# Retention and a Gelu MLP on one core: constants made earlier, seven warm-up matmuls, one load moved ahead, and a choice of queue for the last stores

## The chip, the cores and the metric

The kernel runs on one core of a Trainium2 chip. The metric is the device time of one execution in microseconds (us). The core has a matrix engine (TensorE, PE in the profile, with its weight loads shown apart as PEld), three engines for elementwise work (VectorE as DVE, ScalarE as ACT, GpSimd as POOL) and SyncE (SP), which here only issues transfers. Each engine runs its own list of instructions in a fixed order and waits on semaphores for the others.

## The reference

Inputs are q, k and v of shape (batch 8, heads 8, sequence 576, head size 64) and two weight matrices, 512 x 2048 and 2048 x 512, all float32. Each head is retention without a softmax: scores with a decay by distance, below the diagonal only. The heads side by side form 4608 rows of 512, which go through an MLP with an exact Gelu.

```python
scores = scale * np.matmul(q, k.transpose(0, 1, 3, 2))
gamma = 1.0 - 2.0 ** (-5.0 - np.arange(H, dtype=np.float32))
Dmat = np.where(rel >= 0, gamma[:, None, None] ** rel[None, :, :], 0.0)
x = rows_of(np.matmul(scores * Dmat, v))          # (4608, 512)
out = gelu_exact(x @ w_in) @ w_out                # (4608, 512)
```

## The kernel before, in words

The sequence is cut in chunks of 128 positions, with a last chunk of 64. A unit is one chunk of one batch element, or two last chunks of 64 together; there are 36 units of 128 rows. For a unit, q and k are turned to have the head dimension on the partitions (`qkT`), the scores are taken per head in PSUM (`sc`), VectorE multiplies them by a mask (`ret`, line 452), and a matmul with v gives the unit's result (`o_ps`, line 489). From the second chunk on, an accumulated state of k and v (`u_ps`, `u_sb`) is multiplied by q and added (line 560). First chunks use masks `near` that hold the decay itself. Later chunks use a plain 0/1 mask `msk`, with v scaled by `dv` (`vh`, line 463) and the result by `dqT` (line 583). Four units make a block `x` of 512 tokens, of which there are nine.

The MLP of a block is a first layer (`hT`, line 603, then Gelu into `g_all`) and a second layer (`oT`, line 636, or `fa` and `fb`, line 707). From the second block on the second layer, and for the last three blocks the first layer too (`ha`, `hb`, line 812), use Strassen-like sums with seven products in place of eight, whose operands VectorE prepares (`s`, `wt`, `ws`, `x_sum`).

The order of every engine's instructions is fixed while the program is written, by a planner in the kernel. It keeps an estimated clock per engine (the dictionary `T`), estimated landing times of transfers (`land`), and a main loop that picks what TensorE does next: attention steps that are estimated as ready come first, and otherwise pieces of the MLP. So a changed estimate near the start can move matmuls of the MLP ahead of or behind attention steps much later. Where nothing is estimated as ready before 16 us, `warm(n)` (line 1020) puts matmuls on a tile of zeros into the gap; lines 1048 to 1051 put eight of them ahead of everything.

What the change touches lies at the two ends:

- Lines 108 to 110 load q and k of the first unit as float32, q by SyncE's queue and k by ScalarE's. They are cast to bf16 by VectorE (line 333 is the helper that records such copies on VectorE, line 335 on ScalarE). All other loads are issued by GpSimd in the order of the list `ORDER` (line 281): `wi` is a piece of w_in (256 columns), `wo` a piece of w_out, `q1`, `k1`, `v1` belong to unit 1, and `io` stands for the constants' positions.
- `constants()` makes `val`, `far`, the eight `near` tiles (by exponentials on ScalarE, line 154) and `ident`. The rest (`make_args`, `make_msk`, the exponentials `dv` and `dqT`, and one Gelu on a single column that loads ScalarE's table) lies in a list `later`, from which the main loop takes an item when its planned time has come (lines 174 to 184 and 996 to 1003).
- `put()` (line 1014) issues the stores of a finished tile of 128 rows on SyncE's queue. A unit made of two last chunks has two stores of 64 rows each.

Of the kernel before, what the change touches and what calls it, by code (L numbers as in the profile page):

```python
# [11 lines left out]
AF = mybir.ActivationFunctionType  # L12
# [5 lines left out]
def kernel(  # L18
# [14 lines left out]
    nc = tc.nc  # L33
    ctx.enter_context(tc.manual_schedule())

    B, H, S, D = q.shape
# [3 lines left out]
    scale = 1.0 / math.sqrt(D)  # L40
    HP = H // 2
# [4 lines left out]
    N_BLK = n_tok // TOK  # L46
# [23 lines left out]
    N_LD = 5  # L70
    N_QKT = 3
    N_KN = 4
    VH_POOL = 26
    N_VH = 6
    N_XB = 4
# [3 lines left out]
    HOT = 7.5  # L79
# [16 lines left out]
    T = dict.fromkeys(("pe", "act", "dve", "pool", "sp"), 0.0)  # L96
# [11 lines left out]
    for nm, src, eng in (("q32", q, nc.sync), ("k32", k, nc.scalar)):  # L108
        t = first[nm] = o_pool.tile([128, H, D], FP32, tag="o_sb", name=nm)
# [6 lines left out]
    ln_scale = const.tile([128, 1], FP32, name="ln_scale")  # L116
# [13 lines left out]
    pe_arg = const.tile([128, H, NCI], FP32, name="pe_arg")  # L130
    dv = const.tile([128, H, NCI], FP32, name="dv")
    off = const.tile([128, HP, 1], FP32, name="off")
    dqT = const.tile([128, HP, S - C], FP32, name="dqT")
    warm_act = const.tile([128, 1], FP32, name="warm_act")
# [10 lines left out]
    def constants():  # L145
        nc.gpsimd.iota(val[:, 0, :], pattern=[[1, 128]], base=0, channel_multiplier=-1,
                       allow_small_or_imprecise_dtypes=True)
        nc.gpsimd.iota(pos[:, 0, :], pattern=[[C, NCI]], base=0, channel_multiplier=1,
                       allow_small_or_imprecise_dtypes=True)
        at = on("pool", 0.45)  # L150
        nc.vector.tensor_scalar(far, val, 0.0, 1.0e6, op0=ALU.is_lt, op1=ALU.mult)
        nc.vector.tensor_tensor(far, far, val, op=ALU.add)
        for h in range(H):
            nc.scalar.activation(near[:, h % 2, h // 2], far[:, 0, :], AF.Exp, scale=log_gamma[h], bias=ln_scale)
        nc.vector.tensor_scalar(ident, val, 0.0, None, op0=ALU.is_equal)
        T["act"] = at + 0.6 + H * 0.27
        T["dve"] = at + 0.9

    ident1 = ident[:, 0, :]

    def make_args():
        nc.vector.tensor_scalar(pos[TAIL:, :, NCI - 1:], pos[TAIL:, :, NCI - 1:], float(-TAIL), None, op0=ALU.add)
        nc.vector.tensor_tensor(pe_arg, lgh.to_broadcast([128, H, NCI]), pos.to_broadcast([128, H, NCI]), op=ALU.mult)
        nc.vector.tensor_tensor(off, lgT, pos[:, :, 1:2].to_broadcast([128, HP, 1]), op=ALU.mult)
# [6 lines left out]
    def make_dq(hp):  # L171
        nc.scalar.activation(dqT[:, hp, 0:C], val[:, 0, :], AF.Exp, scale=lgT[:, hp], bias=off[:, hp])

    later = [(7.6, "dve", 0.45, make_args), (7.6, "dve", 0.6, make_msk),
             (8.5, "act", 0.3, lambda: nc.scalar.activation(dv, pe_arg, AF.Exp, scale=-1.0, bias=ln_scale))]
    later += [(9.0, "act", 0.41, lambda hp=hp: make_dq(hp)) for hp in range(HP)]
    later += [(9.0, "act", 1.45, lambda: nc.scalar.activation(warm_act, ln_scale, AF.Gelu))]
    T["act"], T["dve"], T["pool"] = 2.6, 2.9, 0.85

    def finish_later():  # L180
        while later:
            _, engine, dur, fn = later.pop(0)
            fn()
            on(engine, dur)
# [6 lines left out]
    land = {}  # L191
# [37 lines left out]
    def load(what, i):  # L229
# [37 lines left out]
        for jj in (j,) if j is not None else range(2):  # L267
# [5 lines left out]
            else:  # L273
# [2 lines left out]
            land[what, i] = sw_dma(0.9, 0.9) if j is not None else sw_dma(0.68, 0.5)  # L276

    tiles_of(0)
    land["q", 0], land["k", 0] = 4.5, 4.6
    cast_due = {("q", 0): (loaded[0][0][:, 0], first["q32"]), ("k", 0): (loaded[0][0][:, 1], first["k32"])}  # L280
    ORDER = ("wi0 io k1 q1 v0 v1 wi1 q2 k2 v2 wi2 k3 q3 v3 wi3 wi4 wi5 wi6 wi7 wo0 wo1 wo2 wo3 wo4 wo5 wo6 wo7 "
             "q4 k4 q5 k5 v4 v5 dq2 q6 k6 q7 k7 v6 v7 q8 k8 q9 k9 v8 v9 dq3 q10 k10 v10 dq4 q11 k11 q12 k12 n11 n12 v11 v12").split()

    def next_order():
# [39 lines left out]
    def pe(dur, to="full"):  # L324
        if mode[0] != to:
            T["pe"] += 0.11
            mode[0] = to
        T["pe"] += dur * (2.0 if T["pe"] < HOT else 1.0)
        return T["pe"] + DRAIN
# [125 lines left out]
            s["ret"].append(r)  # L455

    def scaled_v(i):
        if len(later) > HP + 1:
            finish_later()
        ci = units[i][1]  # L460
        vh = vh_pool.tile([128, H, D], BF16, tag="vh", name="vh")
        on_pool = i >= VH_POOL
        (nc.gpsimd if on_pool else nc.vector).tensor_tensor(vh, loaded[i][1], dv[:, :, ci:ci + 1].to_broadcast([128, H, D]), op=ALU.mult)
        st[i]["vh"] = vh
        st[i]["V"] = (on("pool", 1.0, land["v", i]) if on_pool else on("dve", 0.7, land["v", i])) + SEM
# [133 lines left out]
    def mlp1(t, m0, n, lo, hi):  # L599
        b, hT = bank([128, n, hi - lo], FP32, "hT")  # L600
        for m in range(m0, m0 + n):
            for cc in range(N_DM):
                nc.tensor.matmul(hT[:, m - m0, :], lhsT=w_in[:, cc, m * 128:m * 128 + 128], rhs=x_tiles[t][:, cc, lo:hi],  # L603
                                 start=(cc == 0), stop=(cc == N_DM - 1))
        done = pe(n * N_DM * ((hi - lo) / 2400 + 0.0025))
        finish_later()
        if hi - lo == TOK:
            nc.scalar.activation(g_all[:, t % 2, :, m0, :], hT.rearrange("p n (a c) -> p (n a) c", a=2), AF.Gelu)  # L608
        else:
            lo_ = lo % (TOK // 2)  # L610
            nc.scalar.activation(g_of(t, 2 * lo // TOK)[:, m0:m0 + n, lo_:lo_ + hi - lo], hT, AF.Gelu)  # L611
        done = on("act", act_dur(n * (hi - lo)), done)
        for m in range(m0, m0 + n):
            for ts in range(lo // 128, hi // 128):
                g_at[t, m, ts] = done + SEM
        release(b, done + 0.05)


    def rows_of(t, ts):
        bp, ci, j = units[t * 4 + ts]  # L620
        if j is not None:
            return [((2 * bp + j) * S + ci * C, 0, C)]
        return [((2 * bp + jj) * S + ci * C, TAIL * jj, TAIL) for jj in range(2)]
# [251 lines left out]
    runs1, runs2 = [], []  # L875
# [23 lines left out]
    def left(runs, t):  # L899
        return sum(len(r) for u, r in runs if u == t)  # L900
# [64 lines left out]
    def side_jobs(now):  # L965
# [4 lines left out]
        idle = T["dve"] <= now + SLACK  # L970
        if nV < min(N_U, len(s_done) + N_VH) and land.get(("v", nV), 1e9) + 0.1 <= now and (nV < nA or nV >= VH_POOL):
            if idle if nV < VH_POOL else T["pool"] <= now + 0.5:
# [16 lines left out]
    def fire():  # L989
        now = T["pe"]  # L990
        while ORDER and T["pool"] <= now + 1.5:
            next_order()
        for key in [x for x in cast_due if land[x] <= now + 0.2]:
            dst, src = cast_due.pop(key)
            land[key] = either(0.44, 0.6, land[key], dst, src) + SEM
        while later:
            n = next((n for n, x in enumerate(later) if x[0] <= now and T[x[1]] <= now + 0.05
                      and (x[1] == "dve" or later[0][3] is not make_args)), None)
            if n is None:
                break  # L1000
            _, engine, dur, fn = later.pop(n)
            fn()
            on(engine, dur, now)
        if FAST2 and not wt and not wsum and len(land_out) == N_DF // 2 and max(land_out.values()) <= now and {0, 1, 2, 3} <= s_done:
            wsum.extend(w_out_sums())
        while True:
            jobs = side_jobs(now)
            if not jobs:
                break
            min(jobs, key=lambda x: x[0])[1]()  # L1010
        while stores and stores[0][0] <= now + 0.2:
            put()

    def put():
        ready, t, ts, o_sb, lo, hi = stores.pop(0)
        for row, p0, n in rows_of(t, ts):
            nc.sync.dma_start(out[row:row + n, lo:hi], o_sb[p0:p0 + n, lo:hi])
        sw[0] += 0.7 * (hi - lo) / d_model

    def warm(n):  # L1020
        b, t = bank([128, 512], FP32, "warm")
        for _ in range(n):
            nc.tensor.matmul(t, lhsT=zeros[:, :128], rhs=zeros, start=True, stop=True)
        pe(0.2158 * n)
        release(b, T["pe"])

    def attend(n):
# [17 lines left out]
        nT += half == 0  # L1045

    T["pe"] = 1.3
    for _ in range(8):
        b, t = bank([128, 512], FP32, "warm")
        nc.tensor.matmul(t, lhsT=zeros[:, :128], rhs=zeros, start=True, stop=True)  # L1050
        release(b, 0.0)
    T["pe"] = 4.9
    while True:
        fire()
        now = T["pe"]
# [14 lines left out]
        if nB < nA:  # L1070
            n = group_of[nB]
# [9 lines left out]
        if nA < N_U:  # L1081
            n = group_of[nA]
# [18 lines left out]
        if due:  # L1101
# [5 lines left out]
            elif kind == "S":  # L1107
                n = group_of[nA]
# [28 lines left out]
        if not waits:  # L1137
            break
        gap = min(waits) - now
        if now < 16 and gap > 0.2:  # L1140
            warm(max(1, round(gap / (0.43 if now < HOT else 0.23))))
        T["pe"] = max(T["pe"], min(waits))
    while stores:
        put()
# [31 lines left out]
```

## Time and profile before

| what | us |
|---|---|
| median of three runs (300.61, 300.78, 299.72) | 300.61 |
| the profiled execution, its own time | 299.83 |
| its span in the profile | 298.1 |
| TensorE busy in the span | 285.2 (96%) |
| VectorE busy | 231.2 (78%) |
| GpSimd busy | 158.2 (53%) |
| ScalarE busy | 135.9 (46%) |

The span begins with the first instruction of the program and ends with the last; 1.7 us of the execution's own time lie around it. The profile gives, for each instruction, its start from the beginning of the span, its duration, how long its engine had been idle before it, and what ended that idle time. A matmul's record includes the time that its result takes to leave the array, so that records of back-to-back matmuls overlap, and the rate is read from their starts.

### The profile page before, as it was taken

Reading aid. Unit: us, or ns where it says so; the run is one execution under the profiler, and the core shown is the slowest. Engines: PE = TensorE matmul, PEld = TensorE weight load, DVE = VectorE, ACT = ScalarE, POOL = GpSimd, SP = SyncE. Lnnn points to the kernel's source line nnn. Section 1 sums busy time; section 2 is a strip of 40 time slices with the busy share of each in tenths; the row PEclk is TensorE's granted clock in tenths of the full one; section 3 lists DMA queues with packets and bytes.
Section 4 is the critical chain, followed back from the end, with each engine's and each line's share of the span. In section 5 each row is a group of like instructions: output and inputs, shape, how many; then the busy total and the mean of one; then the engine's idle time right before and its main releaser. Section 6 shows DMA issues by size and latency. Waiting matters only on the chain.

```text
span 298.1 us, 8709 instructions
## 1 busy us (share of the span) xinstructions
PE 285.2 (96%) x3693; PEld 211.5 (71%) x3720; DVE 231.2 (78%) x430; ACT 135.9 (46%) x262; POOL 158.2 (53%) x231
## 2 busy tenths in 40 slices
PE   7999999998999999999999999999999999999994
PEld 2578656887756656766666656567888888888883
DVE  3872039999999999996770699847997999898851
ACT  5546315844254354343445433534453555546421
POOL 8976798899999988989889941000000000000000
PEclk9999999999999999999999999999999999999998
DMA  9999999999999999999999610201001201201114
GB/s 141 168 186 204 182 170 189 166 135 131 121 162 135 138 141 150 110 160 120 192 151 132 78 38 2 73 2 37 35 2 70 74 0 73 71 2 62 45 55 124
DMA packets 111415, 31.50 MB, mean 106 GB/s; under 512 B 89105, under 2 KB 107025, under 8 KB 111377
## 3 DMA queue, kind: packets, MB, share of 16 engines
q0 software_dynamic: 103744, 20.99, 83.8%
q1 hardware_dynamic: 6592, 9.70, 9.6%
q8 instruction: 29, 0.48, 0.6%
q10 hardware_dynamic: 1040, 0.26, 0.4%
q14 instruction: 10, 0.07, 0.1%
HBM read 42.47 MB, written 9.44 MB: 174 GB/s over the span
## 4 chain that ended last, share of the span: by engine, by line
PE 46%; POOL 24%; DMA 13%; DVE 9%; issue 5%; ACT 1%; DVEq 0%; POOLq 0%; ACTq 0%
PE fa L707 13%; POOL qkb_ld L261 11%; PE fb L707 10%; PE hT L603 7%; PE ha L812 7%; DMA qk_ld<-in_q_dram 6%; PE hb L812 5%; POOL v_ld L275 5%; DMA qkb_ld<-in_q_dram 3%; DMA w_out<-in_moe_w_out_dram 3%; POOL early L275 3%; DVE ret L452 2%; POOL w_in L234 2%; DVE qkT L380 2%; DVE s L675 1%
## 5 line engine op out<-in xcount | busy, mean ns | idle before, releaser
L603 PE MATMUL hT<-x,w_in 128*128 128x512 bf16 (+2 forms) x522 | 92.2, 314 | 2.0 <-DVE x L333 0.5
L603 PEld LDWEIGHTS <-w_in 128*128 128x128 bf16 x544 | 49.4, 98 | 24.5 <-issue 0.9
L707 PEld LDWEIGHTS <-g_all 128*128 128x128 bf16 x512 | 49.5, 98 | 11.6 <-issue 0.7
L608 ACT ACTIVATE g_all<-hT 128x512 bf16<-128x512 f32 x64 | 38.1, 597 | 42.6 <-PE hT L603 40.0
L707 PEld LDWEIGHTS <-s 128*128 128x128 bf16 x384 | 37.0, 98 | 8.3 <-issue 0.3
L693 DVE TENSOR_TENSOR o_sb<-fb,t 128x256 f32<-128x256 f32 x48 | 19.9, 416 | 22.3 <-ACT t L335 11.7
L817 ACT ACTIVATE g_all<-tt 128x512 bf16<-128x512 f32 x36 | 22.6, 630 | 30.2 <-DVE tt L825 30.1
L261 POOL DMA_DIRECT2D qkb_ld<-in_k_dram x56 | 31.1, 594 | 5.6 <-DMA v_ld<-in_v_dram 2.6
L707 PE MATMUL fa<-w_out,g_all 128*128 128x256 bf16 x256 | 33.1, 273 | 0.1
L452 DVE TENSOR_TENSOR ret<-sc,msk 128x512 bf16<-128x512 f32 x48 | 29.6, 671 | 2.8 <-PE sc L425 1.7
L261 POOL DMA_DIRECT2D qkb_ld<-in_q_dram x56 | 31.1, 593 | 0.3 <-issue 0.3
L275 POOL DMA_DIRECT2D v_ld<-in_v_dram x36 | 30.4, 862 | 1.4 <-DMA w_out<-in_moe_w_out_dram 0.8
L825 DVE TENSOR_TENSOR tt<-hb,tt 128x512 f32<-128x512 f32 x36 | 24.5, 687 | 5.2 <-ACT tt L335 2.8
L611 ACT ACTIVATE g_all<-hT 128x512 bf16<-128x512 f32 (+1 forms) x36 | 19.4, 549 | 14.4 <-PE hT L603 14.2
L380 DVE STREAM_TRANSPOSE qkT<-qkb_ld 128x512 f32<-128x512 f32 (+1 forms) x28 | 25.0, 945 | 0.0
L335 ACT COPY t<-fa 128x256 f32<-128x256 f32 x35 | 13.0, 371 | 21.1 <-PE fa L707 21.1
L275 POOL DMA_DIRECT2D kn_ld<-in_k_dram x22 | 19.8, 907 | 2.0 <-DMA qkb_ld<-in_q_dram 1.1
L812 PEld LDWEIGHTS <-ws 128*128 128x128 bf16 x192 | 18.8, 98 | 2.2
L583 DVE TENSOR_TENSOR x<-o_ps,dqT 128x512 bf16<-128x512 f32 (+1 forms) x32 | 18.2, 608 | 1.2 <-PE o_ps L560 1.2
L333 DVE COPY qkT<-qk_ps 128x512 bf16<-128x512 bf16 x10 | 3.9, 419 | 17.4 <-PE qk_ps L368 17.4
L707 PE MATMUL fa<-wt,g_all 128*128 128x256 bf16 x128 | 16.5, 273 | 0.2 <-ACT t L335 0.2
L707 PE MATMUL fb<-w_out,s 128*128 128x256 bf16 x128 | 16.4, 273 | 0.2
(112 smaller groups left out, 455.3 us busy)
## 6 DMA issues: line engine op xcount, KB each, us to landing
out_dram<-o_sb SPq DMA_DIRECT2D x31, 256.0 KB, 2.7
v_ld<-in_v_dram POOLq DMA_DIRECT2D x28, 128.0 KB, 4.7
qkb_ld<-in_q_dram POOLq DMA_DIRECT2D x44, 64.0 KB, 4.2
qkb_ld<-in_k_dram POOLq DMA_DIRECT2D x44, 64.0 KB, 3.7
kn_ld<-in_k_dram POOLq DMA_DIRECT2D x22, 128.0 KB, 4.3
w_in<-in_moe_w_in_dram POOLq DMA_DIRECT2D x8, 256.0 KB, 6.9
w_out<-in_moe_w_out_dram POOLq DMA_DIRECT2D x8, 256.0 KB, 10.0
out_dram<-o_sb SPq DMA_DIRECT2D x8, 128.0 KB, 3.0
```

The costliest lines, as they stand in the source:

```text
L261: nc.gpsimd.dma_start(qk[p0:p0 + 32, "qk".index(what), 0:HP * per].rearrange("p (h x) -> p h x", h=HP), {"q": q, "k": k}[what][2 * bp + jj ...
L275: nc.gpsimd.dma_start(dst, src[2 * bp + jj, :, ci * C:ci * C + n, :].rearrange("h s d -> s h d"))
L380: nc.vector.transpose(dst, src)
L452: nc.vector.tensor_tensor(r, t, by, op=ALU.mult)
L603: nc.tensor.matmul(hT[:, m - m0, :], lhsT=w_in[:, cc, m * 128:m * 128 + 128], rhs=x_tiles[t][:, cc, lo:hi], start=(cc == 0), stop=(cc == N ...
L608: nc.scalar.activation(g_all[:, t % 2, :, m0, :], hT.rearrange("p n (a c) -> p (n a) c", a=2), AF.Gelu)
L611: nc.scalar.activation(g_of(t, 2 * lo // TOK)[:, m0:m0 + n, lo_:lo_ + hi - lo], hT, AF.Gelu)
L693: nc.vector.tensor_tensor(dst, src, f[key], op=ALU.add)
L707: nc.tensor.matmul(dst, lhsT=x[:, kk, :], rhs=y[:, kk, :], start=(name in "125" and kk == 0), stop=(kk == HK - 1), skip_group_check=True)
L812: nc.tensor.matmul(dst[:, m, :], lhsT=a[:, cc, c0:c0 + 128], rhs=y[:, cc, :], start=(name in "125" and m == 0 and cc == 0), stop=(cc == HC ...
L817: nc.scalar.activation(g_of(t, part)[:, m0:m0 + 2], src, AF.Gelu)
L825: nc.vector.tensor_tensor(f[key], f["b"][1], f[key], op=ALU.add)
```

## The change

Four things are edited, and the planner's estimates with them.

- `constants()` now calls `make_args` and issues `dv` and `dqT` itself, right behind the eight `near` tiles. Of the list `later` two items remain: the Gelu that loads the table (from 7.3 us of the planner's clock, now the first item) and `make_msk` (from 24 us). `finish_later` gets a flag, by which a first-layer piece of the MLP does not force `make_msk`.
- Seven warm-up matmuls stand at the start instead of eight, and the planner counts a cold warm-up as 0.64 us (twice 0.32) instead of 0.43 us.
- `v0` moves ahead of `k1` and `q1` in `ORDER`. The landing times assumed for the first q and k are changed.
- `put()` chooses ScalarE's queue for the second store of 64 rows in the last block, if no piece of that block's second layer is left to place.

```diff
+    N_WARM = 7
+    MSK_AT = 24.0
@@ constants()
-        T["act"] = at + 0.6 + H * 0.27
-        T["dve"] = at + 0.9
+        make_args()
+        nc.scalar.activation(dv, pe_arg, AF.Exp, scale=-1.0, bias=ln_scale)
+        for hp in range(HP):
+            make_dq(hp)
+        T["act"], T["dve"] = 7.5, 4.05
@@
-    later = [(7.6, "dve", 0.45, make_args), (7.6, "dve", 0.6, make_msk),
-             (8.5, "act", 0.3, lambda: nc.scalar.activation(dv, pe_arg, AF.Exp, scale=-1.0, bias=ln_scale))]
-    later += [(9.0, "act", 0.41, lambda hp=hp: make_dq(hp)) for hp in range(HP)]
-    later += [(9.0, "act", 1.45, lambda: nc.scalar.activation(warm_act, ln_scale, AF.Gelu))]
+    later = [(7.3, "act", 1.45, lambda: nc.scalar.activation(warm_act, ln_scale, AF.Gelu)), (MSK_AT, "dve", 1.0, make_msk)]
@@
-    def finish_later():
-        while later:
+    def finish_later(fine=True):
+        while later and (fine or later[0][3] is not make_msk):
@@
-    land["q", 0], land["k", 0] = 4.5, 4.6
+    land["q", 0], land["k", 0] = 4.65, 5.2
-    ORDER = ("wi0 io k1 q1 v0 v1 wi1 q2 k2 v2 ...
+    ORDER = ("wi0 io v0 k1 q1 v1 wi1 q2 k2 v2 ...
@@ scaled_v()
-        if len(later) > HP + 1:
-            finish_later()
@@ mlp1()
-        finish_later()
+        finish_later(False)
@@ fire()
-            n = next((n for n, x in enumerate(later) if x[0] <= now and T[x[1]] <= now + 0.05
-                      and (x[1] == "dve" or later[0][3] is not make_args)), None)
+            n = next((n for n, x in enumerate(later) if x[0] <= now and T[x[1]] <= now + 0.05), None)
@@ put()
-        for row, p0, n in rows_of(t, ts):
-            nc.sync.dma_start(out[row:row + n, lo:hi], o_sb[p0:p0 + n, lo:hi])
+        for m, (row, p0, n) in enumerate(rows_of(t, ts)):
+            queue = nc.scalar if t == N_BLK - 1 and m and not left(runs2, t) else nc.sync
+            queue.dma_start(out[row:row + n, lo:hi], o_sb[p0:p0 + n, lo:hi])
@@ warm()
-        pe(0.2158 * n)
+        pe((0.32 if T["pe"] < HOT else 0.2158) * n)
@@
-    for _ in range(8):
+    for _ in range(N_WARM):
...
-    T["pe"] = 4.9
+    T["pe"] = 1.3 + 0.62 * N_WARM
@@ the main loop's fill of a gap
-        if now < 16 and gap > 0.2:
-            warm(max(1, round(gap / (0.43 if now < HOT else 0.23))))
+        if now < 16 and gap > (0.6 if now < HOT else 0.2):
+            warm(int(gap / 0.6) if now < HOT else max(1, round(gap / 0.23)))
```

In the order that the planner makes of this, TensorE has seven warm-ups instead of nine ahead of the first transposes, and 22 instead of 24 in all. The results of units 0 and 2 swap engines, as do copies of several turned tiles. Between about 40 and 180 us pieces of the MLP stand at other places among the attention steps. TensorE's list is the same from there to the end, and so is the whole list of SyncE: all stores stay on its queue, and ScalarE's list has no store.

## The prediction

> **What bounds the kernel now.** I read the busy shares first, then the busy time by stretch, then TensorE's and VectorE's instructions in the order of time at the start, and TensorE's waits.
>
> ```profile
> PE 285.2 (96%) x3693; PEld 211.5 (71%) x3720; DVE 231.2 (78%) x430; ACT 135.9 (46%) x262; POOL 158.2 (53%) x231
> ```
> ```profile
> 44.00:60.00 16.00, 15.38 (x216) 11.40 (x203) 16.00 (x27) 10.59 (x22) 14.29 (x22) 1.00 1.82 178
> 134.00:167.00 33.00, 32.74 (x331) 21.90 (x320) 16.38 (x28) 14.97 (x29) 29.93 (x46) 1.00 1.39 140
> 260.00:280.00 20.00, 20.00 (x185) 17.92 (x184) 17.56 (x33) 11.15 (x20) 0.00 (x0) 1.00 0.09 31
> ```
> ```profile
> 1.19 5.09 PE L1050 MATMUL warm<-zeros 128*128 128x512 bf16 x8 [1.19 <-DVE zeros L112]
> 6.34 0.58 PE L1023 MATMUL warm<-zeros 128*128 128x512 bf16 x1
> 6.71 1.06 PE L368 MATMUL qk_ps<-ident,early 128*128 128x128 bf16 x8
> 8.29 0.61 PE L391 MATMUL sc<-qkT 64*128 64x128 bf16 x8
> 8.83 1.14 PE L1023 MATMUL warm<-zeros 128*128 128x512 bf16 x4
> ...
> 11.79 1.24 PE L1023 MATMUL warm<-zeros 128*128 128x512 bf16 x5 [0.16 <-issue]
> 12.87 0.61 PE L603 MATMUL hT<-x,w_in 128*128 128x128 bf16 x8
> ```
> ```profile
> 4.67 0.83 DVE L333 CAST early<-q 128x512 bf16<-128x512 f32 x1 [1.12 <-DMA q<-in_q_dram]
> 5.43 0.41 DVE L333 CAST early<-k 128x512 bf16<-128x512 f32 x1
> ...
> 11.66 0.79 DVE L169 COPY msk<-msk 64x64 f32<-64x64 f32 x2
> 12.47 0.69 DVE L463 TENSOR_TENSOR vh<-early,dv 128x512 bf16<-128x512 bf16 x1
> 13.08 1.28 DVE L452 TENSOR_TENSOR ret<-sc,near 128x512 bf16<-128x512 f32 x2
> ```
> ```profile
> PE sc L407 <- DVE qkT L380: 2.0, 3, 1.2
> PE o_ps L560 <- ACT u_sb L521: 0.3, 1, 0.3
> ```
>
> The first fence says TensorE is full. The second (stretch; its length; busy time of PE, PEld, DVE, ACT, POOL) says that VectorE is as full as TensorE from 44 us (16.00 of 16) to about 134, and has half its time free after that. The third shows that before 12.87 us TensorE has no MLP work at all: warm-ups fill a chain of load, cast, transpose, copy, scores, mask. All useful matmuls stay the same, so the time is the length of this start, plus fixed work, plus waits, plus an end.
>
> **The change part by part.** *Constants.* `make_args` (0.15 + 0.20 + 0.16) goes into VectorE's idle 1.12 us before the cast at 4.67. `dv` and `dqT` (0.33 + 1.64), then the table load and Gelu (1.28 + 0.20), follow `near`, which ends at 5.62: about 9.0 with their overlaps, inside ScalarE's idle 5.41 us up to 11.03. `msk` (0.22 + 0.79) goes to about 24 us, where VectorE is 2.86 of 10 us busy. All cost nothing there; what they held up is counted below. Were that cover gone, the cost would be their 0.5 to 1.0 us, bounded below by 0.
>
> *Warm-ups and the first unit.* The cold warm-ups start 0.64 apart, so the seventh ends at 5.64. The q cast ends at 5.51, k at 5.84. Transposes start at 5.70 instead of 6.71, and 1.01 is gained, not 1.28, because they now share the warm-ups' bank. Copies (0.42 each) end at 7.22, scores start at 7.28 instead of 8.29, masking (1.29) runs 8.00 to 9.29 instead of 9.01 to 10.30.
>
> *v0 ahead of k1 and q1.* Loads issued at 2.57, 3.50 and 4.37 landed 5.3, 5.3 and 5.4 later. q1 goes from the second slot to the third, so it lands at about 9.72 instead of 8.85; its transposes start at 9.80 (before 9.81): the gain is held here. The first unit's `o_ps` now follows directly, 10.05 instead of 10.57, and VectorE copies x by 11.2 (ScalarE before, 11.61). k1's transposes come after it, and the copies now lie on ScalarE (0.58 to 0.60 instead of 0.42): done at 11.41, so scores of unit 1 come at 11.5, 0.26 later than the 11.24 of before.
>
> *Then the gain comes back.* The first MLP piece needs a w_in piece issued at 6.30 that lands 5.4 later, 11.7: it starts at 11.8 instead of 12.87. Masking of unit 1 starts at 11.97 instead of 13.08, since `msk` and `vh` no longer stand ahead of it. Its x is done (ScalarE, free of the table load) at 14.37 instead of 15.89, and the next MLP piece starts at 14.6 instead of 15.95. Unit 2's scores come at 15.5 instead of 17.36; its successor's q (issued 11.27, landing 6.1 later, 17.34) holds TensorE for 0.24; x of unit 2 is done at 18.72 and the MLP goes on at 18.8 instead of 20.34. The fifth piece of w_in (issued 13.74, 7.3 later: 21.0) is then the limit: 21.07 instead of 22.55. From there TensorE is dense. Sum of the start: **-1.45**. Bounds: -1.0 (the step of the first transposes alone) and -1.65 (the largest shift in the chain).
>
> *40 to 134 us.* The first scores with `msk` stand 0.86 us of MLP earlier in the new order, so VectorE's full stretch begins 1.45 + 0.86 = 2.3 earlier than its 43.73. At 72.64 TensorE waited 1.21 for VectorE's transposes; these scores stand 0.87 earlier in the order, so VectorE's lead is worth 2.3 - 0.87 = 1.43, what the start gave. On the way a wait of some 1.4 appears at about 58.7 (`o_ps` stands 2.6 us of MLP earlier than before, VectorE's masking only 1.4), and the one at 72.64 goes for it. At 118.38 (wait 0.33) a load decides: GpSimd issued k at 113.13, landing 3.2 later, and of the waits in its chain only the 0.62 at 89.53 was for VectorE; so 115.7 to 116.3, plus the transpose (1.10): scores at about 116.9, -1.5. So here -0.05; bounds: +1.4 (the new wait stays on top) and -0.85 (all of the 2.3 arrives).
>
> *167 to 188 us.* The wait of 0.34 at 183.01 was for `u_sb`, behind a state step that now stands 4.3 us of MLP earlier. I take -0.30; bounds +0.4 (a like wait elsewhere) and -1.1 (all waits between 172 and 188: 0.21, 0.36, 0.34, 0.17).
>
> *Stores.* SyncE's list is the same, so 0. The condition asks that nothing of the last block is left to place, and the second stores of 64 rows are placed while the last product still is. Had it worked, the bound is 0.6, from VectorE's end at 294.17 to the last issue at 294.79.
>
> Sum: -1.45 - 0.05 - 0.30 = **-1.8**. Against the profiled execution's 299.83 (span 298.1 plus 1.7) that is 298.0, against the median of 300.61, 0.78 above it, 298.8. I apply it to the mean of the four times, 300.24: **298.4**.
>
> **The rivals.**
>
> *The lead of VectorE carries* (-2.6): its 2.3 arrives whole and the 0.34 goes too. For it: 19.62 to 19.96 of every 20 us are VectorE's between 60 and 120. Against: the load at 113.13. 297.6.
>
> *The middle gives it back* (-0.35): the wait of 1.4 at 58.7 stays on top. For it: attention steps stand up to 2.6 us of MLP earlier while GpSimd's loads follow at their own pace. Against: VectorE was the limit there already. 299.9.
>
> *The full rate comes later* (slower). The cold warm-ups start 0.64 apart, those from 9.17 on 0.22; so the full rate came at about 9.0. With fewer warm-ups it could come after the first MLP piece, at 12.3. Then three warm-ups cost 0.63 more ahead of q1's transposes, these and `o_ps` and k1's 0.5, four warm-ups 0.85, scores and first MLP piece 0.65: +2.6, net +0.8, 301.0. It ends slower if the rate changes later than about 11.5. Against: from 5.7 to 9.1 the new order holds TensorE as long as the old (transposes 0.85, scores 0.55, warm-ups 1.7 against 0.85 + 0.55 + 1.5).
>
> The Trainium skill, TensorE: Matmul & The Clock Gate, Part 1, says the gate opens after a busy window of about 3.4 us that runs free of the kernel's start, and Part 4 that transposes don't count as busy; by it a missed window costs 3.4 us at half rate. The trace agrees that there is one step, at about 9.0; where the window lies in other runs it does not show.
>
> *The stores do nothing*: taken as certain above, and in the sum.
>
> **How the numbers follow.** Half a per cent (1.5 us) is about what a measurement of this kernel can tell from no change. My sum: 0.55, its own range 297.4 to 299.4, two thirds of it beyond 1.5. VectorE's lead: 0.15. Given back: 0.17. Late rate: 0.10, most of it within reach of +0.5%. Several waits at once: 0.03. Faster 0.55 x 0.67 + 0.15 = 0.52; slower 0.10, from the last two, whose upper end adds a new wait of 1.4 to the late rate's +0.8; the rest 0.38. The range runs from 297.0 (the lead with the larger late bound) to 300.9 (up to the late rate).
>
> **What would show it.** In the profile after: first transposes at 5.7, the first MLP piece at 11.8, the first masked scores on VectorE at about 41.4 instead of 43.73, a wait of TensorE near 58.7 and none of 1.2 near 70, no wait for `u_sb`, the last MLP matmul about 1.8 earlier, and the same 4.4 us from it to the span's end. Matmuls 0.64 or 0.43 apart beyond 9.5 us would speak for the late rate. Wrong would be: q1 later than 9.8, or waits above 4 us in sum between 25 and 190.

## The result, and the profile after

The changed kernel is slower. Seven runs gave 301.60 us as the median (300.94 to 302.72), the kernel before on the same chip 300.19; the ratio is 1.0045 with an interval of 1.0033 to 1.0057, so about +1.35 us where -1.8 was forecast. The profiled execution is the slowest of the seven, 302.72 (span 300.6); against the 299.83 of the profile before it is 2.9 us longer, and 1.1 of that is above its own median, while the profile of before lies 0.4 below its. So the two profiles show more loss than there is at the median, and what is read from them is held against runs of other kernels below.

The busy shares of the changed kernel, and its rows for the transfers in 40 slices of 7.5 us (busy share of the 16 DMA engines, which carry out the transfers, in tenths, and GB/s moved):

```profile
PE 284.4 (95%) x3688; PEld 211.1 (70%) x3718; DVE 231.6 (77%) x429; ACT 136.2 (45%) x263; POOL 158.5 (53%) x231
...
DMA  9999999999999999999999720201001201201014
GB/s 148 165 188 204 179 183 171 145 132 135 119 101 172 143 123 152 106 147 131 167 130 189 64 76 2 72 2 37 35 2 70 73 0 72 70 2 71 36 55 124
```

TensorE's busy time is nearly the same (285.2 before), so the longer span is waiting. The row to remember is DMA: the transfers are busy from the start to 165 us. The page of before has the same row up to there, and the prediction did not read it.

TensorE and VectorE at the start of the changed kernel (start, duration, instruction, in brackets the idle time and what ended it):

```profile
1.19 4.45 PE L1050 MATMUL warm<-zeros 128*128 128x512 bf16 x7 [1.19 <-DVE zeros L114]
5.70 1.01 PE L370 MATMUL qk_ps<-ident,early 128*128 128x128 bf16 x8
...
7.23 0.61 PE L393 MATMUL sc<-qkT 64*128 64x128 bf16 x8
...
11.69 0.62 PE L603 MATMUL hT<-x,w_in 128*128 128x128 bf16 x8
...
14.38 1.04 PE L603 MATMUL hT<-x,w_in 128*128 128x256 bf16 x8 [0.16 <-issue]
```
```profile
4.56 0.43 DVE L335 CAST early<-q 128x512 bf16<-128x512 f32 x1 [0.52 <-DMA q<-in_q_dram]
5.16 0.53 DVE L335 CAST early<-k 128x512 bf16<-128x512 f32 x1 [0.18 <-DMA k<-in_k_dram]
...
11.79 1.29 DVE L454 TENSOR_TENSOR ret<-sc,near 128x512 bf16<-128x512 f32 x2 [0.82 <-PE sc L393]
12.99 0.68 DVE L463 TENSOR_TENSOR vh<-early,dv 128x512 bf16<-128x512 bf16 x1
```

The start came as forecast: transposes at 5.70 (forecast 5.70, before 6.71), the first MLP piece at 11.69 (11.8, before 12.87), the second at 14.38 (14.6, before 15.95). The constants are done by 8.88 and hold nobody up.

The stretches that the prediction showed, now after (stretch; length; busy PE, PEld, DVE, ACT, POOL; TensorE's granted clock, DMA share, GB/s), and TensorE's waits (sum, count, longest):

```profile
44.00:60.00 16.00, 14.14 (x201) 10.14 (x201) 16.00 (x25) 9.35 (x20) 15.01 (x23) 1.00 1.92 158
134.00:167.00 33.00, 32.74 (x346) 21.85 (x350) 18.29 (x32) 14.27 (x28) 30.39 (x45) 1.00 1.50 146
260.00:280.00 20.00, 20.00 (x186) 17.90 (x184) 17.76 (x33) 11.45 (x22) 0.00 (x0) 1.00 0.17 54
```
```profile
PE sc L409 <- DVE qkT L382: 1.6, 3, 0.6
...
PE sc L409 <- DVE u_acc L519: 1.0, 3, 0.5
PE hT L603 <- DVE x L583: 0.9, 2, 0.7
PE qk_ps L370 <- DMA qk_ld<-in_q_dram: 0.8, 2, 0.5
PE hT L603 <- DMA w_in<-in_moe_w_in_dram: 0.7, 1, 0.7
```

From 134 us on TensorE is as busy as before. Between 44 and 60 TensorE is busy 14.14 of 16 us instead of 15.38. Waits for VectorE's `u_acc` and for loads are new; the three for `qkT` remain and are smaller (1.6 in all, 2.0 before).

At the first matmul of the second layer (line 636) the changed kernel is 0.8 us ahead (31.86, before 32.65); at the last wait of both (232.28, before 230.04) it is 2.2 behind. Two places carry this loss: TensorE's waits of 0.15 and more sum to 2.6 between 30 and 70 us (before 0.5), and to 3.4 between 70 and 131 (before 2.2). First, TensorE between 38 and 54 us, where only waits are shown:

```profile
40.14 1.17 PE L370 MATMUL qk_ps<-ident,qk_ld 128*128 128x128 bf16 x16 [0.35 <-DMA qk_ld<-in_q_dram]
...
46.27 0.61 PE L370 MATMUL qk_ps<-ident,qk_ld 128*128 128x128 bf16 x8 [0.49 <-DMA qk_ld<-in_q_dram]
47.16 0.61 PE L370 MATMUL qk_ps<-ident,qk_ld 128*128 128x128 bf16 x8 [0.29 <-DMA qk_ld<-in_k_dram]
...
52.94 1.03 PE L603 MATMUL hT<-x,w_in 128*128 128x256 bf16 x8 [0.75 <-DVE x L583]
```

Here TensorE stands at q of unit 5 and at q and k of unit 7 until they land (40.01, 46.13 and 47.03). The wait of 0.75 is for VectorE. Second, between 70 and 130 us:

```profile
72.11 0.32 PE L479 MATMUL o_ps<-ret,vh 64*64 64x64 bf16 x16 [0.51 <-DVE vh L463]
73.12 0.64 PE L409 MATMUL sc<-qkT 32*128 32x128 bf16 x32 [0.57 <-DVE qkT L382]
81.41 0.62 PE L409 MATMUL sc<-qkT 32*128 32x128 bf16 x29 [0.54 <-DVE u_acc L519]
90.20 0.61 PE L409 MATMUL sc<-qkT 32*128 32x128 bf16 x29 [0.21 <-DVE u_acc L519]
101.93 0.64 PE L409 MATMUL sc<-qkT 32*128 32x128 bf16 x32 [0.48 <-DVE qkT L382]
120.47 0.62 PE L409 MATMUL sc<-qkT 32*128 32x128 bf16 x29 [0.28 <-DVE u_acc L519]
129.33 0.64 PE L409 MATMUL sc<-qkT 32*128 32x128 bf16 x32 [0.53 <-DVE qkT L382]
```

These sum to 3.12; the kernel before had three there (1.21 at 72.64, 0.51 at 107.03, 0.33 at 118.38), 2.05. All are waits for VectorE.

### The profile page after: what moved, and what is told of

Read it like the earlier page. It is cut to its first block, busy times and chain, and to the rows that moved or that the text cites. A ratio compares the mean times of both kernels' runs of the same rounds, so it can differ in the third digit from the quotient of the medians.

```text
span 300.6 us, 8705 instructions
## 1 busy us (share of the span) xinstructions
PE 284.4 (95%) x3688; PEld 211.1 (70%) x3718; DVE 231.6 (77%) x429; ACT 136.2 (45%) x263; POOL 158.5 (53%) x231
## 3 DMA queue, kind: packets, MB, share of 16 engines
HBM read 42.47 MB, written 9.44 MB: 173 GB/s over the span
## 4 chain that ended last, share of the span: by engine, by line
PE 39%; POOL 27%; DMA 22%; issue 8%; DVE 2%; ACT 1%; POOLq 0%; DVEq 0%; ACTq 0%
PE fa L707 12%; POOL qkb_ld L263 10%; DMA v_ld<-in_v_dram 9%; PE fb L707 9%; PE ha L812 7%; POOL v_ld L277 6%; PE hb L812 5%; PE hT L603 5%; DMA w_out<-in_moe_w_out_dram 4%; DMA qkb_ld<-in_q_dram 3%; POOL early L277 3%; DMA w_in<-in_moe_w_in_dram 3%; POOL kn_ld L277 3%; DMA qk_ld<-in_k_dram 3%; POOL qk_ld L277 1%
## 5 line engine op out<-in xcount | busy, mean ns | idle before, releaser
L608 ACT ACTIVATE g_all<-hT 128x512 bf16<-128x512 f32 x64 | 38.1, 598 | 43.2 <-PE hT L603 39.2
L707 PE MATMUL fb<-w_out,g_all 128*128 128x256 bf16 x128 | 16.6, 273 | 0.0
```

Of the source, the lines that this page charges most:

```text
L707: nc.tensor.matmul(dst, lhsT=x[:, kk, :], rhs=y[:, kk, :], start=(name in "125" and kk == 0), stop=(kk == HK - 1), skip_group_check=True)
```

## The experiments

Three theories stood after this. **Order:** the planner puts the attention steps of the middle at other places, and that costs. **Loads:** an earlier start meets loads that do not come earlier. **VectorE:** it takes the start's gain, whatever the loads do. Order and loads are undone alone, and together. Ratios are against the kernel before, which ran beside each group at 300.34 to 300.45.

### The two halves of the change apart: start and order of the middle

The planner's clock is nudged once, which leaves the start and GpSimd's list of loads as they are and moves only the middle. In the changed kernel:

```diff
+    turn_at = [25]
     while True:
+        if turn_at and T["pe"] > turn_at[0]:
+            turn_at.clear()
+            T["pe"] += 0.2
         fire()
```

> The changed kernel with one edit to its planner: its estimated TensorE clock is put 0.2 us later once, when it first passes 25 us. The start, the constants, v0's place and GpSimd's whole list of loads stay those of the changed kernel; between 40 and 178 us the attention steps then stand at the same places among the MLP pieces as in the kernel before (only the scores of units 29 and 31 differ, by 0.9 to 1.7 us of MLP). Theory 1, the order of the middle costs the time: the start's lead, 0.5 us of MLP work at 25 to 30 us in the traces, stays and the loss goes, so 0.3 to 0.8 below the kernel before, some 299.7. Theory 2, the loads decide (they land later by 0.8 to 1.9 from 15 us on whatever the order of the matmuls): it stays at +1.0 to +1.4, some 301.5. Theory 3, the traced delay of the loads is a matter of that one execution and the start's gain is lost to VectorE: within 0.3 of the kernel before.

Measured: ratio 1.0003 (0.9986 to 1.0020), 300.14. The loss of 1.35 goes, but the start's gain does not appear. This is what the third theory said; the first had forecast 0.3 to 0.8 below the kernel before.

In the kernel before the same lines with -0.2:

> The kernel before with one edit to its planner: its estimated TensorE clock is put 0.2 us earlier once, when it first passes 25 us. The start, the constants, ORDER and GpSimd's whole list are those of the kernel before; between 40 and 180 us the attention steps stand at the places of the changed kernel (but for four of them, by 0.9 to 1.7 us of MLP). Theory 1, the order of the middle costs the time: the loss of the changed kernel without its start's gain, +1.5 to +2.2, some 302.0. Theory 2, the loads decide: 0, some 300.2, since no load is moved. Theory 3: within 0.3 of the kernel before.

Measured: ratio 1.0063 (1.0051 to 1.0075), +1.9 us. No load and nothing of the start is moved here, so the order alone costs this (the lists of VectorE and ScalarE change with TensorE's: VectorE, for one, now copies a turned tile at 55.83). TensorE's waits in this kernel:

```profile
71.61 0.32 PE L479 MATMUL o_ps<-ret,vh 64*64 64x64 bf16 x16 [0.95 <-DVE vh L463]
72.62 0.64 PE L407 MATMUL sc<-qkT 32*128 32x128 bf16 x32 [0.57 <-DVE qkT L380]
80.92 0.61 PE L407 MATMUL sc<-qkT 32*128 32x128 bf16 x29 [0.55 <-DVE u_acc L519]
89.71 0.61 PE L407 MATMUL sc<-qkT 32*128 32x128 bf16 x29 [0.21 <-DVE u_acc L519]
101.44 0.64 PE L407 MATMUL sc<-qkT 32*128 32x128 bf16 x32 [0.48 <-DVE qkT L380]
120.02 0.63 PE L407 MATMUL sc<-qkT 32*128 32x128 bf16 x29 [0.28 <-DVE u_acc L519]
128.87 0.64 PE L407 MATMUL sc<-qkT 32*128 32x128 bf16 x32 [0.51 <-DVE qkT L380]
```

They are the waits of the changed kernel at the same instructions, wait for wait: 3.55 in all against 2.05, so 1.5 of the 1.9 is seen directly. They belong to the order, whatever stands ahead of it.

### Parts of the change alone, and undone

Seven warm-ups in the kernel before, nothing else (`for _ in range(8)` becomes `range(7)`, and the planner's start of 4.9 is kept):

> The kernel before with seven warm-ups issued instead of eight, and nothing else: the planner's clock starts at 4.9 as before, so every later instruction of every engine keeps its place. The first transposes can start 0.3 to 0.6 earlier (the q cast ended at 5.51, the warm-up behind them stays). The prediction's sum would give -0.3 to -0.6 at the first transposes, held at 9.8 by q1's landing and then by dv, msk and vh: between 0 and -0.3 at the end, some 300.0. Theory 1 (order): the same, since the order is that of before. Theory 2 (loads): 0, as no load moves. A late clock would show as matmuls 0.64 apart beyond 9.5 us and +0.3 or more.

Measured: 0.9997 (0.9988 to 1.0007). The first second-layer matmul (line 636) starts at 31.77 instead of 32.65; nothing of that 0.9 arrives at the end. TensorE waits for no load of note in this trace (0.16 at 43.38); the 0.9 goes at VectorE, as is shown below.

v0 put back behind k1 and q1 in the changed kernel:

```diff
-    ORDER = ("wi0 io v0 k1 q1 v1 ...
+    ORDER = ("wi0 io k1 q1 v0 v1 ...
```

> The changed kernel with ORDER of the kernel before (k1 and q1 ahead of v0): the move of v0 alone is undone. The planner then gives the middle the places of the kernel before (units 3, 4 and 6 by 0.5 to 0.9 us of MLP later, unit 29 by 1.8). Theory 1 (order): the start's lead is kept, so 0.3 to 0.9 below the kernel before, some 299.6. Theory 2 (loads): if v0's place is what delays the later loads, the same 299.6; if it is that the loads are issued some 0.9 earlier, +1.0 to +1.4 as in the changed kernel, and v2 lands 2.5 us behind its neighbour again. Theory 3: within 0.3 of the kernel before.

Measured: 0.9996 (0.9982 to 1.0009). This start is the best of all, the first second-layer matmul at 30.32, 2.3 earlier than before; q1 lands at 8.88 (9.51 in the run with the old middle, but 8.87 in the changed kernel's own profile, so v0's place does not settle it). And then, TensorE:

```profile
46.33 0.61 PE L370 MATMUL qk_ps<-ident,qk_ld 128*128 128x128 bf16 x8 [2.56 <-DMA qk_ld<-in_q_dram]
```

One wait for q of unit 7 takes all of it in this execution, which is the slowest of its twelve: 301.30, at a mean granted clock of 0.994, against a median of 299.98. The others have no trace; the run with q earlier, below, has the same start and shows smaller waits.

v0 first as the only change to the kernel before:

> The kernel before with v0 ahead of k1 and q1, alone. The planner's estimates then give the middle nearly the order of the changed kernel (the same places for units 4 to 20, three or four steps near unit 8 and units 22 to 26 differ by 0.9 to 1.8 us of MLP). If the order of the middle costs the time: +1.2 to +2.2, some 302.0, and the changed kernel's waits at about 72, 81, 102 and 129. If the order costs only together with the earlier constants or fewer warm-ups: within 0.4 of the kernel before.

Measured: 1.0101 (1.0079 to 1.0122), +3.0, more than was expected, and as a test of the order it is inconclusive: most of the loss lies ahead of the middle. The first second-layer matmul is at 35.57, 2.9 late. ScalarE, and the wait that it causes on TensorE:

```profile
10.91 1.64 ACT L172 ACTIVATE dqT<-val,off,lgT 128x128 f32<-128x128 f32 x4
12.57 1.28 ACT L177 ACT_TABLE_LOAD   x1
...
14.43 0.59 ACT L335 COPY qkT<-qk_ps 128x512 bf16<-128x512 bf16 x1
```
```profile
15.07 0.40 PE L391 MATMUL sc<-qkT 64*128 64x128 bf16 x8 [3.09 <-ACT qkT L335]
```

The copy of a turned tile now falls to ScalarE and stands behind `dqT` and the table load. With the constants made early this wait is not there, so v0 first needs them. The wait is not the whole loss: from 15.44 us on TensorE's granted clock is 0.50 for 3.41 us. Of the executions that the ratio takes, four show a mean granted clock of 0.993 to 0.994 and took 303.69 to 303.94; the fifth, at 1.0, took 301.77.

The whole change with eight warm-ups (`N_WARM = 8`):

> The whole change with eight warm-ups in place of seven, one number. The planner's clock then starts 0.62 later, and the middle comes out in the order of the kernel before (units 4 and 6 by 0.9 us of MLP later, unit 29 by 1.8). If the order of the middle is the loss: within 0.5 of the kernel before, some 300.2, without the waits at 81 and 129, though TensorE starts 0.6 later than in the changed kernel. If it is the constants or v0: as the changed kernel or slower, 301.5 to 302.2.

Measured: 1.0006 (0.9992 to 1.0021). One warm-up more, 0.6 us more of planned start, and the loss is gone, since the planner falls back to the old order; the waits at 81 and 129 are absent and those at 72.66, 107.06 and 118.41 are 1.21, 0.50 and 0.33, as before.

### Do the loads hold the earlier start?

The next three leave out half of the columns of w_out's pieces 4 to 7, so that what follows lands earlier (the last piece by 1.9 to 3.0 us in the traces). Every engine's list is unchanged but for one instruction of 0.91 us on VectorE, which fills the rest of w_out with zeros at 22 to 25 us:

```diff
+            w = d_model // 2 if i >= 4 else d_model
-            nc.gpsimd.dma_start(w_out[:, 2 * i:2 * i + 2, :], moe_w_out[i * 256:(i + 1) * 256, :]...
+            nc.gpsimd.dma_start(w_out[:, 2 * i:2 * i + 2, 0:w], moe_w_out[i * 256:(i + 1) * 256, 0:w]...
```

In the kernel with k1 and q1 first, then in the kernel before as the control, then in the changed kernel:

> The kernel of the run with k1 and q1 first, and of w_out's pieces 4 to 7 only half of the columns is loaded (the other half of w_out is filled with zeros by VectorE at about 24 us, so part of the second layer is left out); every engine's list is otherwise the same. That kernel had 2.3 us of MLP work more than the kernel before at 25 to 43 us and lost all of it by 46, in a wait of 2.56 us for q of unit 7. The four pieces landed 1.25 apart, so what is behind them lands up to 2.5 earlier. Theory A, the queue of loads is full from 6 to 45 us and holds back any earlier start: 1.0 to 2.3 below the kernel before, some 298.6, and no wait for a load between 40 and 55. Theory B, VectorE, full from 44 us on, takes the lead whatever the loads do: within 0.4 of the run without the halving, some 300.0.

> The control: the kernel before with the same halves of w_out left out, all lists otherwise unchanged. Its TensorE waits for no load between 25 and 60 us, and its q of unit 7 lands 0.7 us ahead of its use. Theory A: 0 to -0.4, as its start sets when it asks for the loads; theory B: 0. A gain of more than 0.8 here would say that fewer bytes help in some other way (later loads, memory traffic) and would take the verdict from the run with k1 and q1 first.

> The changed kernel with the columns of w_out's pieces 4 to 7 halved as in the runs before (half of w_out is zeros, part of the second layer is left out), every engine's list otherwise that of the changed kernel. Its loads behind them land up to 2.5 us earlier, so its waits for loads at 40, 46 and 47 us (1.1 in all) go and what is left against the kernel before is the start's gain, 0.5 at 25 us, and the order of the middle, +1.5 to +1.9. Theory: slower than the kernel before by +0.3 to +1.4 still, some 301.2, with the same waits of 0.5 at about 72, 73, 81, 101 and 129. If the loads were the whole loss of the changed kernel, it would be 0.3 to 0.9 below the kernel before, some 299.8.

| half of the late w_out loads left out in | ratio | interval |
|---|---|---|
| k1 and q1 first | 0.9949 | 0.9937 to 0.9961 |
| the kernel before | 1.0009 | 0.9994 to 1.0023 |
| the changed kernel | 1.0000 | 0.9991 to 1.0009 |

The control gains nothing, so fewer bytes help only a kernel that starts earlier, which the third theory does not allow: -1.4 us for the one with k1 first (0.9996 to 0.9949), -1.35 for the changed one (1.0045 to 1.0000). The last is outside what was expected, +0.3 to +1.4; the loads held more of the changed kernel's time than the 1.1 us of waits for them in its profile, and the two effects do not simply add. Its profile still shows the waits of the new order (0.49, 0.57, 0.54, 0.21, 0.48, 0.28, 0.54 between 70 and 129). Landing times and TensorE's progress, from the traces, us from the span's start:

| | before | after | after, old middle | k1 first | k1 first, half | after, half |
|---|---|---|---|---|---|---|
| last piece of w_out lands | 35.13 | 36.97 | 36.04 | 35.15 | 33.28 | 34.01 |
| q of unit 7 lands | 43.49 | 46.13 | 45.11 | 46.19 | 41.34 | 42.31 |
| first second-layer matmul | 32.65 | 31.86 | 31.36 | 30.32 | 30.52 | 31.31 |
| VectorE's first masking with `msk` | 43.73 | 42.71 | 43.25 | 42.43 | 42.47 | 41.53 |

The loads do not follow the start: nothing that the change does makes the last piece of w_out land earlier. In the kernel before, q of units 5 and 7 land 1.4 us ahead of their transposes (38.12 against 39.55, 43.49 against 44.91; the control's expectation had 0.7), and where the landing stays, a lead beyond that becomes a wait. With the loads out of the way the changed kernel's first masking is at 41.53, where the prediction had 41.4.

A part of the lead goes even then. In the run with k1 first and half loads, TensorE:

```profile
50.30 0.38 PE L371 MATMUL qk_ps<-ident,qk_ld 128*128 128x128 bf16 x4 [0.96 <-DVE u_acc L520]
```

Of 2.1 at the first second-layer matmul, 0.7 is left at the scores of units 11 and 12 (71.92, before 72.64). Here TensorE waits for VectorE, and VectorE for GpSimd. In the kernel before, and with seven warm-ups:

```profile
45.85 1.08 POOL L243 TENSOR_TENSOR dqT<-dqT,step 128x512 f32<-128x512 f32 x1
46.73 0.76 DVE L463 TENSOR_TENSOR vh<-v_ld,dv 128x512 bf16<-128x512 bf16 x1
```
```profile
46.03 1.10 POOL L243 TENSOR_TENSOR dqT<-dqT,step 128x512 f32<-128x512 f32 x1
45.85 1.84 DVE L463 TENSOR_TENSOR vh<-v_ld,dv 128x512 bf16<-128x512 bf16 x1
```

Both `vh` end 0.56 us after `dqT` does. In each of the fourteen traces the last `vh` or `wt` (VectorE's sums of w_out) that meets a `dqT` ends 0.55 to 0.56 after it, however early it began; where it meets none it takes 0.68. Masking, which reads PSUM, keeps its 0.68 beside `dqT`. With seven warm-ups v of units 4 and 5 had landed by 40.94, so the 1.84 holds no wait for a load. `dqT` stands in GpSimd's list behind issues of loads, and the start does not move it forward: 45.85 before, 46.03 with seven warm-ups, 47.17 with the old middle. So a lead of 0.9, less than the 1.4 above, is lost all the same. In the run with k1 first and half loads `dqT` comes at 44.91, `vh` takes 1.17, and part of the lead is left. The halving thus moved two things, the landings and `dqT`; how much each holds was not separated.

### Two attempts to bring the loads forward

In the kernel with k1 and q1 first, q ahead of k within each pair of units:

```diff
-"q4 k4 q5 k5 v4 v5 dq2 q6 k6 q7 k7 v6 v7 q8 k8 q9 k9 ...
+"q4 q5 k4 k5 v4 v5 q6 q7 k6 k7 dq2 v6 v7 q8 q9 k8 k9 ...
```

> The kernel of the run with k1 and q1 first (constants early, seven warm-ups, the order of before in the middle), and q of units 5, 7 and 9 moved one place ahead of k of 4, 6 and 8 in ORDER, v4 and v5 left ahead: q7 lands one load, some 0.6 to 1.0 us, earlier, k6 as much later, and the rest stays. Theory A (loads hold the lead): q7 was the load waited for, so 0.3 to 1.0 below the run with k1 and q1 first, some 299.3. Theory B (VectorE): no difference to it, some 300.0.

Measured: 1.0009 (0.9990 to 1.0028), no gain. In its trace TensorE waits 0.40 for k of unit 7, and then 1.11 for VectorE's `u_acc` at 51.41, behind a `vh` of 2.23 that met `dqT`. And q6, q7 and k6 put ahead of v4, and k7 ahead of v5, with the planner's estimates left alone:

> The kernel of the run with k1 and q1 first, with ten loads issued in another order and every other list unchanged: q6, q7, k6 ahead of v4, k7 ahead of v5 (before: v4, v5, q6, k6, q7, k7; the planner still counts them in that order). q7 lands two or three loads earlier, some 1.6 to 2.5 us, k7 one load. Theory (loads hold the lead at 43 to 50, then VectorE holds it at 50): as in the run with half loads TensorE keeps 0.8 to 1.2 of its lead, 299.0 to 299.6. If v4 and v5, now last, are what VectorE waits for: 300 or above, with a gap of VectorE near 45.

Measured: 0.9996 (0.9984 to 1.0008), a miss. In its trace q7 landed at 41.34, but v4 at 42.76, k7 at 44.87, and TensorE waits 0.40 for `vh` (1.92 long, again with `dqT`) at 48.62 and 0.57 for q of unit 9 at 50.76. An order of loads that keeps the lead was not found.

### The stores

In the kernel before, the second store of each pair of the last block on ScalarE's queue, without the condition on what is left:

```diff
+            queue = nc.scalar if t == N_BLK - 1 and m else nc.sync
```

> The kernel before with the second of each pair of stores of 64 rows of the last block issued by ScalarE, the condition on what is left dropped, so that the choice of queue takes effect. By the prediction's bound the tail can shorten by at most 0.6: 299.7 to 300.4. If the stores' own landing sets the end, 0.

Measured: 0.9976 (0.9968 to 0.9985), 299.67, the best version that computes everything. SyncE's issues at the end before, and SyncE's and ScalarE's here:

```profile
291.12 4.06 SPq L1017 DMA_DIRECT2D out_dram<-o_sb  x7
```
```profile
291.21 3.42 SPq L1018 DMA_DIRECT2D out_dram<-o_sb  x5
...
292.11 1.42 ACTq L1018 DMA_DIRECT2D out_dram<-o_sb  x2
```

The last issue ends 3.42 us after the first instead of 4.06: 0.64 less, and the time falls by 0.7. The gain was there to be had, but the condition in the change is never true.

## Why the prediction was wrong

**"40 to 134 us: -0.05" is the term that failed.** The order of the middle costs +1.9 alone (1.0063), above the term's upper bound of +1.4. The changed kernel with the old middle is back at 1.0003. The prediction saw that steps move by up to 2.6 us of MLP, and priced it as one new wait of 1.4 near 58.7 in place of the one at 72.64. What came is no wait of that size at 58.7 (0.17 at 58.66), the 1.21 turned into 0.51 and 0.57 on neighbouring instructions, and four waits of 0.2 to 0.55 at 81, 90, 120 and 129 that the prediction did not look for: it walked the chain to 72.64 and took one load at 118, and let the rest stand. Which of the moved steps causes which wait was not separated. The prediction's own sign of being wrong, waits above 4 us in sum between 25 and 190, came: those of 0.15 and more are 6.9 in the profile after, where that of before has 3.8.

**"From there TensorE is dense", the end of the start's term.** The instants of TensorE up to 14.4 us were right to 0.3, in part by luck: q1 was to land at 9.72 and the w_in piece of the first MLP matmul at 11.7, but they landed at 8.87 and 10.74, and that matmul came at 11.69 behind the scores of unit 1. The -1.45 behind them was not kept. At the first second-layer matmul 0.8 was left in the profiled execution (1.3 with the old middle), and at the end nothing: 1.0003. The chain used fixed landing times for the loads up to 21 us and then dropped them, though those at 38 and 43.5 us have only 1.4 us to spare. VectorE's lead of 2.3, on which the rest was built, needed q of unit 5 earlier than it comes. Nor did it look at GpSimd's `dqT`, which VectorE's `vh` met already in the kernel before (0.76 instead of 0.68): with seven warm-ups 0.9 of lead goes there, with hardly a wait for a load.

**The mechanism "the middle gives it back"** came nearest among the rivals: -0.35 where it was +1.35. Its wait at 58.7 is not there. It counted a gain kept and one wait added; in truth the gain is lost to GpSimd's pace, that of the loads and of `dqT`, and the order's waits come on top.

**"167 to 188 us: -0.30"** did not come: 0.66 at 175.73 and 0.27 at 176.23 stand for the 0.21, 0.36 and 0.34 of before. The wait for `u_sb` went, and one for ScalarE's `u_acc` took its place: 0.

**Right:** the constants cost nothing where they now lie; the stores do nothing as written, and their bound of 0.6 measured 0.7; the late clock did not happen (the full rate is there from 8.7 us, before 9.1; the whole change with eight warm-ups had it at 11.38 in its trace and still took 299.81). *The lead of VectorE carries* is refuted by the first masking at 42.71 and by the run with the old middle.

## What to carry to other kernels

When a start is shortened, ask at once what does not move with it: the next transfers' landing times and how long they lie ready before their use (here 1.4 us), and work that stands behind the issue of transfers on the same engine (here `dqT`, with next to no slack). Leads of 0.8 to 2.3 us were lost to the two. Where a planner with estimated clocks orders the work, compare the whole order that a small edit produces, and price every step that moves on an engine that is full; a nudge of 0.2 us to the plan was worth 1.9 us here, more than the edit itself.

## What the runs showed of the hardware

A single wait can cost more than itself. In the kernel with k1 and q1 first, TensorE stood still for 2.56 us, and the granted clock then fell for 3.4 us (PEclk is the third column from the end):

```profile
44.00:47.00 3.00, 0.67 (x10) 0.58 (x11) 3.00 (x6) 0.84 (x2) 0.60 (x2) 1.00 2.31 179
47.00:50.40 3.40, 3.40 (x16) 1.79 (x15) 3.40 (x4) 1.90 (x4) 3.40 (x5) 0.51 2.23 178
```

In the second stretch TensorE never pauses, but at a clock of 0.51 it works at half the rate: matmuls of 512 columns start 0.43 apart, and 0.22 apart again from 50.6 us on. With v0 first the same came after the wait of 3.09. The Trainium skill, TensorE: Matmul & The Clock Gate, Part 1, puts the fall to half rate after at least one idle window of about 3.4 us; here TensorE had worked 0.67 us in the three before, and its clock fell all the same.

VectorE's `vh`, a product of two tensors in SBUF, did not end while GpSimd's `dqT`, another one, was running: it took 0.76 to 2.25 us where the two met, the longest where it began ahead of `dqT`, and 0.68 where they did not.

Loads behind the same bytes do not land at the same time in each execution: q of unit 7 came at 43.2 to 46.2 us in the traces with all of w_out loaded and that load at its old place, with GpSimd's issue at 36.8 to 38.7. What holds some of them back by 1 to 3 us was not found.
